# Six idle TensorE products fewer between the phases of the first pair of a fused SSD and FFN kernel

## Chip, cores and metric

The kernel runs on one core of one Trainium2 chip. The metric is the device time of one execution in microseconds (us); the median of five runs is compared. Next to it stands one profiled execution, whose records of every instruction make up the trace.

## What is computed

A Mamba-2 style state-space scan ("SSD") over batch 4, 8 heads, 768 positions, head width 32 and state width 16 is followed by a feed-forward network with squared ReLU. Cut to what matters:

```python
for c in range(S // 32):
    cum = cumsum(log(a[:, :, sl]))
    M   = (C_c @ B_c.T) * exp(cum_i - cum_j) * causal
    y[:, :, sl] = M @ x_c + (C_c @ state) * exp(cum)
    state = exp(cum_last) * state + sum_j(B_j x_j exp(cum_last - cum_j))
x = y.transpose(0, 2, 1, 3).reshape(3072, 256)
h = maximum(x @ w_in, 0)          # 256 -> 2048
out = (h * h) @ w_out             # 2048 -> 256
```

## The kernel before

The 768 positions of each batch element are cut into three stretches of 256. That gives twelve "pairs" (batch, stretch); the kernel numbers them 0 to 11, with all four batch elements of the first stretch first. A pair's SSD output is a tile T (bf16), and the feed-forward network runs over the same 256 positions: for each of eight steps, `mm1` (line 370, four products of 128x256, `hps`) then a ReLU on ScalarE (line 376), a square on VectorE (line 382) and `mm2` (line 400, four products, `ops`). `LAG = 4` steps lie between an `mm1` and its `mm2`.

All instructions are issued in the order in which the source lists them (`tc.manual_schedule()`): each engine goes through its own list strictly in that order, and waits where an operand is not ready. From pair 1 on, the SSD phases of a pair are threaded between the feed-forward steps of earlier pairs by a hand-written table of steps (`at(s, fn, ...)`). Pair 0 has no feed-forward work to stand beside, so its phases run one after another:

- the decays: VectorE scan `cp_r` (line 495), spread over partitions by TensorE products (`ctpt`, `ptr`, `pps`), scaled on VectorE into `bct` (line 526); ScalarE fills the rest of `bct` (line 524)
- `ph_mt(0)` (line 220): 16 products `mt` of B against C, 64x256, eight tiles of the array side by side
- the causal masks of `mt` on VectorE (`ph_mask`, line 231), half of them from a copy that ScalarE makes (`mtc`, line 545)
- `ph_u(0)` (line 249): 16 small products `U` for the carried state; they need `xs`, which GpSimd makes (line 176, `prep_x`)
- `ph_s(0, ...)`: ScalarE scales `U` into the state `Sf` (line 272)
- `ph_y(0)`: 8 products with the state (line 340), which need `Sf`, then 32 products of the masked `mt` with `xs` (line 307, `y_intra`), which need the masks
- two copies turn `Y` into `T0` (line 357), and `ph_tr(1)` starts pair 1 (lines 201 and 203)
- the first `mm1` (line 370)

Between these phases stand idle products, `warm(n, cols)`: n TensorE products of a zeroed tile `dum` with itself, `cols` columns wide, written to a PSUM tile that nobody reads. They wait for nothing and nobody waits for them, but TensorE goes through its list in order, so what is behind them starts only after them. Seven of them stand ahead of everything (lines 488 and 489, six of 512 columns and one of 256), the others are 256 columns wide.

The weights come in pieces on GpSimd's queue: `load_wi(0, 4)` (line 500), then after `prep_x(0)` `load_wi(4, 8)` (line 539), `load_wo(0, 4)` and `load_wo(4, 8)` (lines 548 and 549).

Of the kernel before, what the change touches and what calls it, by code (L numbers as in the profile page):

```python
# [16 lines left out]
def _fap(base: bass.AP, offset_elems: int, free_dims):  # L17

    ap0 = list(base.ap)[0]
    return bass.AP(tensor=base.tensor, offset=base.offset + offset_elems,  # L20
                   ap=[list(ap0)] + [list(d) for d in free_dims])
# [9 lines left out]
def kernel(  # L31
# [94 lines left out]
    def load_wi(f0, f1):  # L126

        for f in range(f0, f1, 2):
            nc.gpsimd.dma_start(  # L129
                out=w_in_b[:, :, f * 128:(f + 2) * 128],  # L130
                in_=_dap(moe_w_in, f * 128, [[2048, 128], [128 * 2048, 2], [1, 256]]))
# [81 lines left out]
    def ph_mt(k):  # L213
        v = live[k]
        bct = v["bct"]
        mt = [ps_s.tile([128, 2, 2, 2, 128], FP32, tag="A", name=f"mt{k}_{i}") for i in range(2)]
        for r in range(2):
            for u in range(2):
                for q in range(4):
                    nc.tensor.matmul(  # L220
                        mt[q // 2][64 * u:64 * u + 64, q % 2, r, :, :],
                        bct[32 * q:32 * q + 32, r, 0, u * 64:u * 64 + 64],
                        _fap(bct[32 * q:32 * q + 32], 128 + u * 64, [[128, 2], [384, 2], [1, 64]]),
                        start=True, stop=True, skip_group_check=True,
                        tile_position=(32 * q, 64 * u))
        v["mt"] = mt
        v["mts"] = big.tile([128, 4, 2, 2, 128], BF16, tag="mts", name=f"mts{k}")

    def ph_mask(k, q, src=None):
        v = live[k]  # L230
        nc.vector.tensor_tensor(  # L231
            out=v["mts"][:, q], in0=v["mt"][q // 2][:, q % 2] if src is None else src,
            in1=_fap(cb, 128, [[128, 2], [0, 2], [1, 128]]), op=ALU.mult)

    def ph_u(k):
        b, j = PAIRS[k]
        v = live[k]
        if k < 1:
            U = [ps_h.tile([128, 64], FP32, tag="hps", name=f"U{k}_{u}", padded_shape=[128, 512])
                 for u in range(2)]  # L240
        else:
            t = ps_s.tile([128, 2, 512], FP32, tag="A", name=f"U{k}")
            U = [t[:, u, 0:64] for u in range(2)]
        for r in range(2):
            for u in range(2):
                if j == 2 and u == 1:
                    continue
                for q in range(4):
                    nc.tensor.matmul(  # L249
                        U[u][32 * q:32 * q + 32, :],  # L250
                        v["Bb"][64 * u:64 * u + 64, r, 32 * q:32 * q + 32],
                        _fap(v["xs"][64 * u:64 * u + 64], r * 256 + q * 32, [[128, 2], [1, 32]]),
                        start=(r == 0), stop=(r == 1), skip_group_check=True,
                        tile_position=(64 * u, 32 * q))
        v["U"] = U
        v["S"] = [state.get(b)]
# [43 lines left out]
    def y_intra(k, Y, first, last):  # L300
        v = live[k]
        for g in range(2):
            for r in range(2):
                for u in range(2):
                    for q in range(4):
                        h = 4 * g + q
                        nc.tensor.matmul(  # L307
                            Y[u][32 * q:32 * q + 32, g, :],
                            v["xs"][64 * u:64 * u + 64, r, h * 32:h * 32 + 32],
                            v["mts"][64 * u:64 * u + 64, q, r, g, :],  # L310
                            start=first[(u, q)], stop=(last and g == 1 and r == 1), skip_group_check=True,
                            tile_position=(64 * u, 32 * q))
                        first[(u, q)] = False
# [3 lines left out]
    def ph_y(k):  # L317
        b, j = PAIRS[k]
        v = live[k]
        if k < 1:  # L320
            Y = [ps_s.tile([128, 2, 128], FP32, tag="A", name=f"Y{k}_{u}", padded_shape=[128, 8, 128])
                 for u in range(2)]
        else:
            t = ps_s.tile([128, 2, 4, 128], FP32, tag="A", name=f"Y{k}")
            Y = [t[:, u, 0:2, :] for u in range(2)]
        first = {(u, q): True for u in range(2) for q in range(4)}
        if 1 <= k < 4:
            y_intra(k, Y, first, False)
        for u in range(2):
            S_b = v["S"][u]  # L330
            if S_b is None:
                continue
            for g in range(2):
                rhs = [128 + g * 128 + u * 64, [[384, 2], [1, 64]]]
                if k >= 4:
                    nc.tensor.matmul(Y[u][:, g, :], S_b[:, g * 128:(g + 1) * 128], _fap(v["bct"], *rhs),  # L336
                                     start=first[(u, 0)], stop=False, skip_group_check=True)
                for q in range(4):
                    if k < 4:
                        nc.tensor.matmul(  # L340
                            Y[u][32 * q:32 * q + 32, g, :], S_b[32 * q:32 * q + 32, g * 32:(g + 1) * 32],
                            _fap(v["bct"][32 * q:32 * q + 32], *rhs),
                            start=first[(u, q)], stop=(k > 0 and g == 1), skip_group_check=True,
                            tile_position=(32 * q, 32 * q))
                    first[(u, q)] = False
        if k == 0:
            warm(2, 256)
        if k == 0 or k >= 4:
            y_intra(k, Y, first, True)
        if 4 <= k < NPAIR - 1:  # L350
            ph_u(k + 1)

        T[k] = tpool.tile([128, 2, 2, 2, 64], BF16, tag="T", name=f"T{k}")
        if k < 1:
            for u in range(2):
                copy = nc.vector.tensor_copy if u else nc.scalar.copy
                copy(out=_fap(T[k], u * 64, [[128, 4], [1, 64]]), in_=_fap(Y[u], 0, [[64, 4], [1, 64]]))
        else:
            nc.scalar.copy(out=_fap(T[k], 0, [[64, 2], [128, 4], [1, 64]]),  # L359
                           in_=_fap(Y[0], 0, [[512, 2], [64, 4], [1, 64]]))  # L360
# [84 lines left out]
    with tc.manual_schedule():  # L445
# [37 lines left out]
        def warm(n, cols=512):  # L483
            for _ in range(n):
                nc.tensor.matmul(idle[-1][:, 0:cols], dum[:, 0:128], dum[:, 0:cols],  # L485
                                 start=True, stop=True, skip_group_check=True)
# [50 lines left out]
        recip(0, 1, 0)  # L537
        prep_x(0, nc.gpsimd)
        load_wi(4, 8)
        warm(2, 256)  # L540
        ph_mt(0)
        warm(6, 256)
        mtc = {k: big.tile([128, 2, 2, 2, 128], BF16, tag="mtc", name=f"mtc{k}") for k in range(2)}
        for i in (1, 0):
            nc.scalar.copy(out=mtc[0][:, i], in_=live[0]["mt"][1][:, i])
# [2 lines left out]
        load_wo(0, 4)  # L548
        load_wo(4, 8)
        ph_u(0)  # L550
        warm(4, 256)
        ph_mask(0, 3, mtc[0][:, 1])
        ph_mask(0, 2, mtc[0][:, 0])
        prep_c(1, nc.vector)
# [3 lines left out]
        ph_s(0, (1,), "z")  # L558
        prep_b(1, nc.scalar)
        ph_y(0)  # L560
        ph_tr(1)
        recip(2, 2, 0)
# [45 lines left out]
        for k in range(2, NPAIR):  # L608
# [26 lines left out]
            else:  # L635
                if k == 4:
                    at(s0 + 4, ph_u, k)
                at(st + (5 if k == 4 else 0), ph_s, k)
            at(yy, ph_y, k)
        waiting = []  # L640
        between = {2: ((ph_u, (1,)), (ph_s, (1, (0,), "S"))), 3: ((ph_y, (1,)),)}
        for s in range(len(steps) + LAG):
            if s == 4:
# [43 lines left out]
```

## Time and profile before

| | us |
|---|---|
| median of five runs | 118.59 |
| the five runs | 117.41, 117.49, 118.59, 119.40, 119.50 |
| profiled execution, whole | 118.61 |
| its span, first to last instruction | 116.9 |

| engine | busy us | share of the span | instructions |
|---|---|---|---|
| TensorE products (PE) | 109.0 | 93% | 1639 |
| TensorE weight loads (PEld) | 88.0 | 75% | 1639 |
| VectorE (DVE) | 86.9 | 74% | 205 |
| ScalarE (ACT) | 76.2 | 65% | 145 |
| GpSimd (POOL) | 39.0 | 33% | 80 |

In the rows of a timeline the first number is the start in us from the span's beginning, the second the time to the end of the row's last instruction; then come engine, line, operation, output and inputs, shape and how many instructions the row stands for. A bracket tells how long the engine had been idle before and what released it. PE rows overlap, since the products are pipelined: a single 128x256 product is shown with 0.27 us, yet the next one starts much earlier, so the rate is read from the starts. The idle products are the rows of line 485 with the output `dps`.

### The profile page before, as it was taken

The page shows a single profiled execution, that of the slowest core. Times are in us where ns is not written, and L with a number is a line of the kernel's source. Part 1 is how long each engine was busy: PE and PEld are TensorE (multiplying, and loading weights), DVE is VectorE, ACT ScalarE, POOL GpSimd, SP SyncE. Part 2 cuts the span into 40 slices and gives each one's busy share as a digit, 9 for nine tenths or more (in the row PEclk, how much of TensorE's full clock was granted, in tenths as well). Part 3 has the DMA queues.
Part 4 walks back from the last instruction along what each step waited for, and adds up shares of the span by engine and source line. Part 5 has one row for each costly group of instructions (what it writes and reads, how often), then busy time and mean ns, then how long its engine had stood idle before and what let it go on. Part 6 is the DMA issues. An engine that isn't in the chain of part 4 may idle for free.

```text
span 116.9 us, 4011 instructions
## 1 busy us (share of the span) xinstructions
PE 109.0 (93%) x1639; PEld 88.0 (75%) x1639; DVE 86.9 (74%) x205; ACT 76.2 (65%) x145; POOL 39.0 (33%) x80
## 2 busy tenths in 40 slices
PE   5989889989999999999999999999999999999940
PEld 2555578777786787887887897887888878889940
DVE  6788936799796998996996976976958939554420
ACT  5465877576787566586576775865865775868710
POOL 4678966148792600431243604306100000000000
PEclk9999999999999999999999999999999999999999
DMA  3999999989899512927628639278050200200211
GB/s 73 192 169 144 148 193 185 190 138 202 151 286 196 104 48 68 208 68 143 149 95 157 95 97 203 42 172 167 11 157 0 83 12 0 93 2 0 90 48 48
DMA packets 50963, 13.53 MB, mean 116 GB/s; under 512 B 44352, under 2 KB 50048, under 8 KB 50944
## 3 DMA queue, kind: packets, MB, share of 16 engines
q1 hardware_dynamic: 46400, 10.98, 44.7%
q0 software_dynamic: 4288, 2.10, 14.3%
q8 instruction: 13, 0.21, 0.8%
q10 hardware_dynamic: 256, 0.18, 0.5%
q14 instruction: 6, 0.05, 0.1%
HBM read 10.64 MB, written 3.15 MB: 118 GB/s over the span
## 4 chain that ended last, share of the span: by engine, by line
PE 84%; DMA 5%; DVE 4%; POOL 2%; issue 0%; DVEq 0%
PE ops L400 35%; PE hps L370 33%; DMA w_out_b<-in_moe_w_out_dram 5%; PE mt L220 3%; PE Y L307 3%; PE dps L485 3%; DVE mts L231 2%; PE Y L336 2%; PE U L249 1%; POOL w_in_b L129 1%; POOL xs L176 1%; PE ctpt L509 1%; PE ops_r L400 1%; DVE bct L526 1%; PE ops L416 1%; PE ops_r L416 1%
## 5 line engine op out<-in xcount | busy, mean ns | idle before, releaser
L376 ACT ACTIVATE hb<-hps 128x512 bf16<-128x512 f32 x96 | 57.6, 600 | 29.9 <-PE hps L370 28.4
L370 PE MATMUL hps<-T,w_in_b 128*128 128x256 bf16 x384 | 57.6, 273 | 0.5 <-DMA w_in_b<-in_moe_w_in_dram 0.3
L400 PE MATMUL ops<-w_out_b,h 128*128 128x256 bf16 x360 | 55.0, 273 | 0.5 <-DMA w_out_b<-in_moe_w_out_dram 0.5
L382 DVE TENSOR_TENSOR h<-hb 128x512 bf16<-128x512 bf16 x96 | 41.2, 450 | 11.1 <-ACT hb L376 10.9
L370 PEld LDWEIGHTS <-w_in_b 128*128 128x128 bf16 x384 | 37.3, 98 | 5.1 <-DMA w_in_b<-in_moe_w_in_dram 0.6
L400 PEld LDWEIGHTS <-h 128*128 128x128 bf16 x376 | 34.5, 98 | 7.1 <-issue 2.6
L231 DVE TENSOR_TENSOR mts<-mt,cb 128x512 bf16<-128x512 f32 x44 | 29.1, 683 | 9.1 <-PE mt L220 9.0
L176 POOL TENSOR_TENSOR xs<-x_nat,Pinv 128x512 bf16<-128x512 f32 x12 | 13.2, 1100 | 10.9 <-DMA x_nat<-in_x_dram 3.2
L145 POOL TENSOR_TENSOR bc<-C_nat,P_sb 128x128 bf16<-128x128 f32 x16 | 6.8, 443 | 24.4 <-DMA C_nat<-in_C_dram 24.4
L293 DVE TENSOR_TENSOR S<-z,Pown 128x256 bf16<-128x256 f32 x16 | 8.1, 506 | 0.5
L485 PE MATMUL dps<-dum 128*128 128x256 bf16 (+1 forms) x25 | 6.3, 366 | 1.3 <-DVE dum L451 1.3
L359 ACT CAST T<-Y 128x512 bf16<-128x512 f32 x11 | 6.4, 585 | 0.4 <-PE Y L340 0.4
L438 ACT COPY osb<-ops 128x512 f32<-128x512 f32 x11 | 6.4, 580 | 0.0
L129 POOL DMA_DIRECT2D w_in_b<-in_moe_w_in_dram x8 | 6.0, 751 | 0.0
L220 PE MATMUL mt<-bct 32*64 32x256 bf16 x192 | 5.1, 280 | 0.5 <-DVE bct L526 0.3
L170 POOL CAST bc<-B_nat 128x128 bf16<-128x128 f32 x16 | 4.8, 326 | 2.0 <-DMA B_nat<-in_B_dram 2.0
L307 PE MATMUL Y<-mts,xs 64*32 64x128 bf16 x384 | 5.2, 219 | 0.0
L485 PEld LDWEIGHTS <-dum 128*128 128x128 bf16 x25 | 2.4, 112 | 3.3 <-issue 1.8
L307 PEld LDWEIGHTS <-xs 64*32 64x32 bf16 x384 | 3.0, 91 | 1.7 <-issue 0.8
L220 PEld LDWEIGHTS <-bct 32*64 32x64 bf16 x192 | 1.9, 102 | 3.2 <-issue 1.7
L286 DVE SCALAR_TENSOR_TENSOR z<-z,Ptot,U 128x64 f32<-128x64 f32 x12 | 3.2, 265 | 0.3 <-PE U L249 0.2
L134 POOL DMA_DIRECT2D w_out_b<-in_moe_w_out_dram x4 | 3.1, 790 | 0.3 <-issue 0.3
(77 smaller groups left out, 56.7 us busy)
## 6 DMA issues: line engine op xcount, KB each, us to landing
x_nat<-in_x_dram SPq DMA_DIRECT2D x12, 256.0 KB, 3.8
out_dram<-osb SPq DMA_DIRECT2D x7, 256.0 KB, 2.8
C_nat<-in_C_dram SPq DMA_DIRECT2D x12, 128.0 KB, 3.0
B_nat<-in_B_dram SPq DMA_DIRECT2D x12, 128.0 KB, 3.2
w_in_b<-in_moe_w_in_dram POOLq DMA_DIRECT2D x8, 128.0 KB, 5.5
w_out_b<-in_moe_w_out_dram POOLq DMA_DIRECT2D x4, 256.0 KB, 5.9
out_dram<-osb SPq DMA_DIRECT2D x8, 128.0 KB, 2.4
bct<-bc SPq DMA_TRANSPOSE x8, 3.5
```

The lines of the kernel that those rows point to most:

```text
L129: nc.gpsimd.dma_start(out=w_in_b[:, :, f * 128:(f + 2) * 128], in_=_dap(moe_w_in, f * 128, [[2048, 128], [128 * 2048, 2], [1, 256]]))
L145: eng.tensor_tensor(out=_fap(bc[k % 3], r * 384 + 128, [[144, 2], [32, 4], [1, 16]]), in0=_fap(loaded[k]["C"], r * 16, [[128, 2], [32, 4], ...
L176: eng.tensor_tensor(out=_fap(xs, 0, [[256, 2], [32, 8], [1, 32]]), in0=_fap(loaded[k]["x"], 0, [[32, 2], [64, 8], [1, 32]]), in1=_fap(Pinv ...
L220: nc.tensor.matmul(mt[q // 2][64 * u:64 * u + 64, q % 2, r, :, :], bct[32 * q:32 * q + 32, r, 0, u * 64:u * 64 + 64], _fap(bct[32 * q:32 * ...
L231: nc.vector.tensor_tensor(out=v["mts"][:, q], in0=v["mt"][q // 2][:, q % 2] if src is None else src, in1=_fap(cb, 128, [[128, 2], [0, 2], ...
L293: nc.vector.tensor_tensor(out=S_n.rearrange("p (g q d) -> p g q d", g=2, q=4), in0=_fap(z, 0, [[32, 2], [0, 4], [1, 32]]), in1=_fap(Pown, ...
L307: nc.tensor.matmul(Y[u][32 * q:32 * q + 32, g, :], v["xs"][64 * u:64 * u + 64, r, h * 32:h * 32 + 32], v["mts"][64 * u:64 * u + 64, q, r, ...
L370: nc.tensor.matmul(hps[:, i, :], w_in_b[:, g, f * 128:(f + 1) * 128], T[blk][:, g].rearrange("p r u t -> p (r u t)"), start=(g == 0), stop ...
L376: nc.scalar.activation(out=hb, in_=hps, func=AF.Relu)
L382: nc.vector.tensor_tensor(out=h2, in0=hb, in1=hb, op=ALU.mult)
L400: nc.tensor.matmul(o[c], h2[:, i, r * 128:(r + 1) * 128], w_out_b[:, f, c * 128:(c + 1) * 128] if len(o) > 1 else w_out_b[:, f, :], start= ...
L485: nc.tensor.matmul(idle[-1][:, 0:cols], dum[:, 0:128], dum[:, 0:cols], start=True, stop=True, skip_group_check=True)
```

## The change

Six of the idle products of 256 columns go: one of two ahead of `ph_mt(0)`, two of six behind it, two of four behind `ph_u(0)`, and one of two inside `ph_y(0)` between the products with the state and those of `y_intra`. Everything else, and its order on every engine, stays.

```diff
@@ ph_y, line 346
         if k == 0:
-            warm(2, 256)
+            warm(1, 256)
         if k == 0 or k >= 4:
             y_intra(k, Y, first, True)
@@ line 537
         recip(0, 1, 0)
         prep_x(0, nc.gpsimd)
         load_wi(4, 8)
-        warm(2, 256)
+        warm(1, 256)
         ph_mt(0)
-        warm(6, 256)
+        warm(4, 256)
@@ line 548
         load_wo(0, 4)
         load_wo(4, 8)
         ph_u(0)
-        warm(4, 256)
+        warm(2, 256)
         ph_mask(0, 3, mtc[0][:, 1])
```

## The prediction

> **What bounds the kernel now.** I read the page's row of the granted clock and its chain of waits first: TensorE (PE) carries 84% of the chain, in the two feed-forward lines above all, so whatever makes the first of these products start later is paid at the end, unless a later wait swallows it. So I went to the timeline of the first 16 us. PE's rows there, with the idle products (`dps`) among them:
>
> ```profile
> 1.26 2.96 PE L485 MATMUL dps<-dum 128*128 128x512 bf16 x7 [1.26 <-DVE dum L451]
> ...
> 6.21 0.38 PE L485 MATMUL dps<-dum 128*128 128x256 bf16 x2
> 6.89 0.42 PE L220 MATMUL mt<-bct 32*64 32x256 bf16 x16 [0.31 <-DVE bct L526]
> 7.25 0.83 PE L485 MATMUL dps<-dum 128*128 128x256 bf16 x6
> 8.11 0.25 PE L249 MATMUL U<-xs,Bb 64*32 64x64 bf16 x16
> 8.30 0.61 PE L485 MATMUL dps<-dum 128*128 128x256 bf16 x4
> 8.87 0.29 PE L340 MATMUL Y<-bct,Sf 32*32 32x128 bf16 x8
> 9.09 0.39 PE L485 MATMUL dps<-dum 128*128 128x256 bf16 x2
> 9.41 0.45 PE L307 MATMUL Y<-mts,xs 64*32 64x128 bf16 x32
> ...
> 10.54 0.60 PE L370 MATMUL hps<-T,w_in_b 128*128 128x256 bf16 x4
> ...
> 12.60 0.61 PE L370 MATMUL hps<-T,w_in_b 128*128 128x256 bf16 x4 [0.34 <-DMA w_in_b<-in_moe_w_in_dram]
> ...
> 15.10 0.60 PE L400 MATMUL ops<-w_out_b,h 128*128 128x256 bf16 x4 [0.49 <-DMA w_out_b<-in_moe_w_out_dram]
> ```
>
> What each real phase waits for, on the other engines:
>
> ```profile
> 5.87 0.88 DVE L526 SCALAR_TENSOR_TENSOR bct<-ctpt,half,P_T 128x256 bf16<-128x256 f32 x2
> 7.00 1.06 POOL L176 TENSOR_TENSOR xs<-x_nat,Pinv 128x512 bf16<-128x512 f32 x1 [0.74 <-DVE Pinv L534]
> 8.50 0.31 ACT L272 ACTIVATE Sf<-U,Ptot 128x64 bf16<-128x64 f32 x1
> 8.64 0.75 DVE L231 TENSOR_TENSOR mts<-mtc,cb 128x512 bf16<-128x512 bf16 x2
> ```
>
> **Two rates of one product.** The seven leading products (six of 512 columns, one of 256, so 13 half-widths) run from 1.26; the weight loads of line 485 start 0.427 us apart there (1.66, 2.09, 2.52, 2.94, 3.37). That is 0.213 us for 256 columns. The six at 7.25 take (0.83 - 0.27) / 5 = 0.11 us each, 0.27 being one product's own length (the page's 273 ns). So this execution ran at half rate first and at full rate by 7.25. The page's clock row, all nines, does not show it; the trace's clock records hold one full-clock stretch, from 4.98 to 117.62 us. In another execution full clock can come at another moment, and no row here shows such a one. The five runs do spread over 2.1 us (117.41 to 119.50), so both cases have to be worked out.
>
> **At full clock, as profiled, each edit costs and brings nothing.** Each group ends before what PE waits for anyway:
> - two ahead of `mt`: 6.21 + 0.22 = 6.43; `bct` is written until 5.87 + 0.88 = 6.75
> - six behind it: 7.25 + 6 x 0.11 = 7.91; `xs` is there at 7.00 + 1.06 = 8.06
> - four behind `U`: 8.30 + 0.44 = 8.74; `Sf` at 8.50 + 0.31 = 8.81
> - two ahead of the masked products: 9.09 + 0.22 = 9.31; the masks at 8.64 + 0.75 = 9.39
>
> So 6 x 0.11 = 0.66 us of PE work goes and 0.66 us of waiting takes its place. The cover is thin (0.07 to 0.32 us), which is why the rate decides. Nothing is queued differently on VectorE, ScalarE, GpSimd or SyncE: no wait is added, no transfer is moved. `xs` hangs on `Pinv`, thus on VectorE, and the weights' issues behind it on GpSimd's list, not on an idle product.
>
> **At half clock throughout the pair, step by step.** I keep the other engines' durations and give PE 0.213 us for each idle product. For `mt` half rate adds between 0 and 0.21 us (16 products of 256 columns on eight tiles are two rounds, each 0.107 longer; at full rate it takes 0.36 from start to the next start, more than its two rounds of 0.11, so issue limits part of it); I take 0.15, so PE is done with `mt` at 7.40 and the masked products could start at 9.41 + 0.15 = 9.56, as VectorE's masks follow `mt`. `U` and the state products (0.19 and 0.22) I leave, being 64 and 128 columns wide; that is low by at most 0.2 together, and equally in both kernels.
> - before `mt`: 6.21 + 0.43 = 6.64, still under 6.75. Removing one: 0.
> - `U` starts at 7.40 + 6 x 0.213 = 8.68 instead of 8.06; with four, at 8.25.
> - `Sf` lets the state products start 0.76 behind `U` (8.11 to 8.87): 9.44 before, 9.01 after. PE itself is free at 8.68 + 0.19 + 4 x 0.213 = 9.72 before and at 8.25 + 0.19 + 2 x 0.213 = 8.87 after. They start at 9.72 and 9.01.
> - the masked products: 9.72 + 0.22 + 2 x 0.213 = 10.37 before; 9.01 + 0.22 + 0.21 = 9.44 after, which then wait for the masks until 9.56.
>
> Sum: 10.37 - 9.56 = 0.81 us earlier, with the waits on `Sf` and the masks as what is late next. The choice for `mt` does not matter: with 0.21 it is 10.43 against 9.62, with 0 it is 10.22 against 9.41. `T`, its copies and the first feed-forward products follow one for one.
>
> **What of it is left at the end.** The 0.81 us has to pass two gates: `w_in` (0.34 us of PE waiting at 12.60) and `w_out` (0.49 us at 15.10). They swallow it if PE arrives early there. At half clock it does not: from 10.54 to 15.10, four groups of line 370 cost 4 x (0.85 - 0.44) = 1.64 more, three idle products 0.31, `mt` and `Y` of pair 1 some 0.3; less the waits of 0.34 + 0.49 and of about 0.2 ahead of `mt`, PE is 1.2 late at the second gate plus what pair 0 left. Then the lead survives. But if full clock comes at a moment of its own and not after so much work, 0.81 us of work at half rate is worth 0.40 at full rate. So an execution with late full clock gains 0.4 to 0.8, one with early full clock 0. Nothing shows which share of runs is late; the median (118.59) is 1.2 above the fastest run, so I count it as late, and as the trace gives the clock a moment I take the lower end of the gain, 0.4: 118.59 - 0.4 = 118.2. The profiled execution (118.61, of which 1.7 lie outside its span) would itself keep its time.
>
> [...] The trace's full clock began 3.7 us after PE's first product and ended 5.1 us after its last (112.5 to 117.62). [...]
>
> **Rivals.**
> - *Nothing happens (118.6).* All executions have full clock by 6 us, as the profiled one; the spread comes from transfers (PE stands 0.83 us at the two gates). For it: every cover above holds at full rate. Against it: 2.1 us is more than both gates together.
> - *Slower: full clock comes later (120.1).* At half clock the new kernel leaves PE idle 0.14 ahead of the state products (9.01 - 8.87) and 0.12 ahead of the masked ones (9.56 - 9.44), where the old one left nothing. If that is too little activity, runs that had full clock near 8 us keep half clock past 15 us. Price: the 1.2 above plus about 0.3 in pair 0: 1.5, so 118.59 + 1.5 = 120.1. It decides once more than half of the executions fall there. For it: PE's first full clock followed nearly gapless work. Against it: a clock that is full is not lost by this, since PE's half-empty last stretch and 5 us of nothing were needed for that, and 0.3 us of gaps is little.
> - *Clearly faster (117.2).* The lead of 0.81 counts in full in the median run, and dense products that start earlier bring full clock earlier, so that two groups of line 370 more run at 0.44 instead of 0.85 us (0.82): 118.59 - 1.6 is 117.0, and I stop a little above, 117.2, near the fastest run shown (117.41). For it: 117.41 exists, so the kernel has such a state. Against it: no row ties the clock's moment to these products.
>
> **How the numbers follow.** Forecast (0 to 0.8 less) 0.29, nothing 0.15, slower 0.30, clearly faster 0.26. A change of over 1% is 1.2 us, about what measuring this kernel can tell from none, given its spread. The first two stay within, and so does a little of each of the others: faster 0.25, same 0.47, slower 0.28. The range reaches from 116.9 (just under the faster case) to 120.1 (the slower case): it leaves out half of the slower case and little else. The likeliest case's own range is 117.8 to 118.6.
>
> **What would show it.** In the changed profile: at full clock, `mt`, `U`, the state products and the masked products start at 6.89, 8.11, 8.87 and 9.41 still, with gaps of PE ahead of them that are 0.1, 0.2, 0.2 and 0.1 longer, and `ops` waits for `w_out` at about 15.1. If idle products stand 0.21 apart after 6 us, the masked products should start at 9.5 to 9.7. The prediction is wrong if idle products stand 0.21 apart where they stood 0.11 apart before and the first product of line 370 starts later than 10.54 for it, or if a phase waits for something not in the lists above.

## Result and profile after

The change makes no difference that these runs can tell: 118.73 us median over 44 runs against 118.59 us over 79 runs of the kernel before, ratio 1.0008 with a 95% interval of 0.9987 to 1.0030. That is between 0.15 us less and 0.36 us more; the 0.4 us less that the prediction named as likeliest is just outside. The medians are over all runs; the ratios here and below compare only the runs that lie within 1.5% of the fastest run of their kernel.

The profiled execution took 117.72 us, its span is 116.0 us. PE's rows in the timeline of its first 15 us, to be laid beside those of before:

```profile
6.02 0.27 PE L485 MATMUL dps<-dum 128*128 128x256 bf16 x1
6.70 0.42 PE L220 MATMUL mt<-bct 32*64 32x256 bf16 x16 [0.41 <-DVE bct L526]
7.06 0.61 PE L485 MATMUL dps<-dum 128*128 128x256 bf16 x4
7.92 0.26 PE L249 MATMUL U<-xs,Bb 64*32 64x64 bf16 x16 [0.25 <-POOL xs L176]
8.11 0.39 PE L485 MATMUL dps<-dum 128*128 128x256 bf16 x2
8.67 0.29 PE L340 MATMUL Y<-bct,Sf 32*32 32x128 bf16 x8 [0.18 <-ACT Sf L272]
8.90 0.28 PE L485 MATMUL dps<-dum 128*128 128x256 bf16 x1
9.11 0.56 PE L307 MATMUL Y<-mts,xs 64*32 64x128 bf16 x32
...
10.35 0.60 PE L370 MATMUL hps<-T,w_in_b 128*128 128x256 bf16 x4
...
14.93 0.60 PE L400 MATMUL ops<-w_out_b,h 128*128 128x256 bf16 x4 [0.66 <-DMA w_out_b<-in_moe_w_out_dram]
```

The six products are gone, and what PE waits for stands in the brackets instead: `xs` (0.25 us idle), `Sf` (0.18), `bct` (0.41 instead of 0.31). From `mt` to the first product of line 370 it is 3.65 us both times (6.89 to 10.54, 6.70 to 10.35). All of it lies 0.19 us earlier because this execution's clock records show full clock from 4.58 us instead of 4.98, so that the products of line 509 ended sooner. At the weights' gate that lead is 0.17 us (14.93 against 15.10).

The 0.9 us between the two profiled spans is not the change's. PE's last product ends at 112.52 us before and at 112.77 after. What follows is the landing of the last stores, by the lists of DMA issues (queue, issues, size of each, us from issue to landing). Before:

```profile
out_dram<-osb ACTq DMA_DIRECT2D x1, 128.0 KB, 3.1
out_dram<-osb SPq DMA_DIRECT2D x2, 64.0 KB, 2.8
```

After:

```profile
out_dram<-osb ACTq DMA_DIRECT2D x1, 128.0 KB, 1.9
out_dram<-osb SPq DMA_DIRECT2D x2, 64.0 KB, 1.7
```

The stores landed 1.1 to 1.2 us faster, in instructions that the change does not touch. A single profiled span is therefore no measure of an edit of this size.

### The profile page after: what moved, and what is told of

It reads as the page before. It is cut to its first block, busy times and chain, and to the rows that moved or that the text cites. A ratio compares the mean times of both kernels' runs of the same rounds, so it can differ in the third digit from the quotient of the medians.

```text
span 116.0 us, 3999 instructions
## 1 busy us (share of the span) xinstructions
PE 108.4 (93%) x1633; PEld 87.6 (75%) x1633; DVE 88.2 (76%) x205; ACT 76.1 (66%) x145; POOL 39.1 (34%) x80
## 4 chain that ended last, share of the span: by engine, by line
PE 81%; DVE 8%; DMA 5%; POOL 2%; issue 1%; DVEq 0%
PE ops L400 34%; PE hps L370 32%; DMA w_out_b<-in_moe_w_out_dram 5%; DVE mts L231 3%; PE mt L220 3%; PE Y L307 3%; PE dps L485 3%; DVE h L382 2%; PE Y L336 2%; POOL w_in_b L129 1%; PE U L249 1%; POOL xs L176 1%; PE ops_r L400 1%; DVE bct L526 1%; PE ops L416 1%; PE ctpt L509 1%
## 5 line engine op out<-in xcount | busy, mean ns | idle before, releaser
L382 DVE TENSOR_TENSOR h<-hb 128x512 bf16<-128x512 bf16 x96 | 43.3, 474 | 11.2 <-ACT hb L376 11.1
L293 DVE TENSOR_TENSOR S<-z,Pown 128x256 bf16<-128x256 f32 x16 | 7.3, 458 | 0.5
L485 PE MATMUL dps<-dum 128*128 128x256 bf16 (+1 forms) x19 | 5.6, 396 | 1.3 <-DVE dum L451 1.3
```

Source lines behind the costliest of these rows:

```text
L293: nc.vector.tensor_tensor(out=S_n.rearrange("p (g q d) -> p g q d", g=2, q=4), in0=_fap(z, 0, [[32, 2], [0, 4], [1, 32]]), in1=_fap(Pown, ...
L382: nc.vector.tensor_tensor(out=h2, in0=hb, in1=hb, op=ALU.mult)
```

## Experiments

My theory was: at full clock the products are hidden; at half clock they delay pair 0 by about 0.8 us; and since the kernel's runs spread over 2 us, a median run is one of the late kind. The result speaks against the last part or against the gain reaching the end. The rivals: half clock does not happen; it happens, but later waits swallow it; the idle products hold the clock and so give as much as they cost.

**Profiling again.** The two kernels unchanged, one more profiled execution of each:

> The kernel before, profiled once more. Theory (full clock comes early as a rule): the six products behind mt stand 0.11 us apart again, the masked products start by 9.6 us. Rival (half clock is common): the products behind mt stand 0.21 apart and the masked products start at 10.2 to 10.5 us.

> The changed kernel, profiled once more. If it has full clock early (4 to 5 us), mt, U, the state products and the masked products start near 6.7, 7.9, 8.7 and 9.1 us again; if full clock comes near 10 us, as in the second profile of before, they start near 7.3, 8.7, 9.5 and 10.1, the masked products 0.6 to 0.8 us earlier than the 10.79 there. In both cases the mm1 products at the seventh step of the second four-step round start between 25.9 and 26.6 us.

The kernel before, in this second profile, had full clock only from 9.87 us (clock records). PE's rows of the timeline:

```profile
7.96 1.46 PE L485 MATMUL dps<-dum 128*128 128x256 bf16 x6
9.35 0.31 PE L249 MATMUL U<-xs,Bb 64*32 64x64 bf16 x16
9.59 0.73 PE L485 MATMUL dps<-dum 128*128 128x256 bf16 x4
10.25 0.29 PE L340 MATMUL Y<-bct,Sf 32*32 32x128 bf16 x8
10.47 0.39 PE L485 MATMUL dps<-dum 128*128 128x256 bf16 x2
10.79 0.42 PE L307 MATMUL Y<-mts,xs 64*32 64x128 bf16 x32
...
15.76 0.61 PE L400 MATMUL ops<-w_out_b,h 128*128 128x256 bf16 x4
```

So half clock through pair 0 does happen. The six idle products take 1.46 us instead of 0.83, no phase waits for its operand any more (no brackets), and the masked products start at 10.79 instead of 9.41, 1.38 late. Nor does PE wait for `w_out`. Yet this execution took 117.95 us, less than the median.

The changed kernel, profiled again, had full clock from 4.54 us and took 117.93 us:

```profile
9.09 0.56 PE L307 MATMUL Y<-mts,xs 64*32 64x128 bf16 x32
...
15.89 0.27 PE L400 MATMUL ops<-w_out_b,h 128*128 128x256 bf16 x1 [1.60 <-DVE h L382]
```

Here the masked products started 1.70 us earlier than in the profile at half clock, and the products of line 400 0.13 us later: PE stood idle for 1.60 us ahead of them. The releaser named is a square, the fourth, which ended at 15.89. But these products read the first step's square, and the first three had ended by 14.45; in the first profile after the change the same products started at 14.93, ahead of the fourth square (15.44 to 15.86). What else they read is `w_out`, and its first piece is the cause: it was issued at 9.27 and landed 6.58 us later, at 15.85, 0.04 us before PE went on. In both first profiles, where the releaser named is `w_out`, PE also went on 0.04 us behind the landing (15.06 and 15.10 before, 14.88 and 14.93 after). The two executions differ by 1.70 us in pair 0 and by 0.02 us at the end.

**Where a delay goes.** From the rows of line 370 in each trace, the start of a step's four products (steps counted from 0), in us:

| execution | masked products | step 0 | step 4 | step 12 | step 14 | last step |
|---|---|---|---|---|---|---|
| before | 9.41 | 10.54 | 15.54 | 23.67 | 26.20 | 109.71 |
| before, second profile (half clock to 9.87) | 10.79 | 11.91 | 16.52 | 24.50 | 26.58 | 110.17 |
| after | 9.11 | 10.35 | 15.36 | 23.35 | 26.34 | 109.96 |
| after, second profile | 9.09 | 10.33 | 16.32 | 24.31 | 26.62 | 110.15 |

The 1.38 us of the half-clock profile are 0.98 behind the weights' gate, 0.83 at step 12 and 0.38 at step 14. The lead of 0.30 that the first profile after the change has in the masked products is 0.32 at step 12 and turns into 0.14 of lag at step 14. Between those steps lies a third gate, the `U` products of pair 2, which wait for VectorE's masks of pair 2 (`U` goes into a PSUM buffer that `mt` held, so the masks must have read it). The row of these products before:

```profile
24.69 0.26 PE L249 MATMUL U<-xs,Bb 64*32 64x64 bf16 x16 [0.42 <-DVE mts L231]
```

In the second profile of before:

```profile
25.08 0.25 PE L249 MATMUL U<-xs,Bb 64*32 64x64 bf16 x16
```

After the change:

```profile
24.83 0.26 PE L249 MATMUL U<-xs,Bb 64*32 64x64 bf16 x16 [0.88 <-DVE mts L231]
```

So PE waited 0.42 us there before, 0.88 us after, and in the half-clock profile not at all. From step 14 to the last step all four take 83.5 to 83.6 us, so nothing more is won or lost there.

**Twice and four times the idle products,** which puts a known delay into pair 0 at full clock:

```diff
-warm(2), mt, warm(6), U, warm(4), state products, warm(2)     # 256 columns each
+warm(4), mt, warm(12), U, warm(8), state products, warm(4)    # e2_double
+warm(8), mt, warm(24), U, warm(16), state products, warm(8)   # e5_quad
```

> The idle products of pair 0 behind the leading seven are doubled (2, 6, 4, 2 become 4, 12, 8, 4), which at full clock is what half clock makes of the old number: 12 x 0.11 = 1.32 us behind mt put U at 8.57 instead of 8.11, the state products at 9.64 and the masked products at 10.30 instead of 9.41 us, 0.89 late. Theory (gates): the waits for w_in (0.34 us at 12.6) and for w_out (0.49 to 0.66 us at 15) swallow most of it, the products of line 400 still start within 0.3 us of 15.1, and the time rises by 0 to 0.3 us (118.6 to 118.9). Rival (one for one): PE is the bound, so the whole 0.89 us is paid: 119.5.

> The idle products of pair 0 behind the leading seven are made four times as many (8, 24, 16, 8). At full clock 24 x 0.11 = 2.64 us behind mt put U at 9.9, the state products at 11.8 and the masked products at 12.9 instead of 9.4 us: 3.5 late. Theory (gates): what PE waits for anyway takes its part once, 0.34 us at w_in, 0.49 to 0.66 at w_out and 0.4 to 0.9 at the masks of pair 2 near 24.7 us, 1.2 to 1.9 in all, and nothing more; so the time rises by 1.6 to 2.3 us (about 120.2 to 120.9). Rival (one for one): 3.5 us are paid. Rival (PE has slack everywhere): under 1 us is paid.

Doubled: 118.71 us, ratio 1.0029 (0.9990 to 1.0068), which is 0.34 us more. The masked products started at 10.61, 1.2 us late, 0.3 more than I had worked out. PE still waited for `w_out`:

```profile
15.94 0.60 PE L400 MATMUL ops<-w_out_b,h 128*128 128x256 bf16 x4 [0.30 <-DMA w_out_b<-in_moe_w_out_dram]
```

That is 0.8 us later than I expected, since the transfer itself took 6.40 us from issue to landing in this execution against 5.58 in the first profile of before: the gate moves from execution to execution by as much as the effect at issue. Four times as many: 120.76 us over four runs, ratio 1.0216 (1.0153 to 1.0280), 2.6 us more (1.8 to 3.3), for 4.2 us in pair 0, where I had worked out 3.5:

```profile
13.60 0.42 PE L307 MATMUL Y<-mts,xs 64*32 64x128 bf16 x32
```

So by the times 1.6 us were swallowed, and the interval allows 0.9 to 2.4. The profiles are sharper: against the first profile of before, the doubled kernel's 1.19 us are 0.25 at step 14 (26.45), and the 4.19 us here are 3.42 (29.62). The start-up thus swallows 0.8 to 1.0 us in each of the three profiles with a delay, less than the 1.2 to 1.9 that I had summed from the gates, and the rest is paid.

**Half clock forced.** Without the seven leading products PE begins at 4.2 to 4.4 us, and full clock comes later (at 10.21 to 13.54 us in the three profiles). With the counts of before, of after, and with none behind them:

```diff
-        warm(6)
-        warm(1, 256)
```

> The seven leading idle products are left out, the others stand as before the change (2, 6, 4, 2). PE's first product is then that of line 509 at about 4.3 us, so full clock should come some 3 us later than the 4.6 to 5.0 us of the two profiles, between 7.5 and 11.5 us. Theory (half clock delays pair 0): idle products stand 0.21 us apart behind mt, U starts at 8.6 to 8.9, the masked products at 10.2 to 10.6 instead of 9.1 to 9.4 us; the time is 0.5 to 1.5 us longer than before. Rival (gates): all of pair 0's delay is swallowed by the wait for w_out at 15: time within 0.3 us of before, even so.

> The same without the seven leading products, with the idle products of the changed kernel (1, 4, 2, 1). Theory (half clock delays pair 0): the masked products start 0.6 to 0.9 us earlier than in the run without leading products and with 2, 6, 4, 2, and the time is 0.4 to 0.8 us shorter than there. Rival (gates): both start the products of line 400 at about 15, and the two times are equal within 0.3 us. [...]

> Neither the seven leading idle products nor the 14 behind them in pair 0. Theory: at half clock the products of the changed kernel end with the waits, so leaving them out moves no phase of pair 0 forward by more than 0.2 us against the run without leading products and with 1, 4, 2, 1 (masked products at 9.9 to 10.2); what is left is the clock: full clock begins later, near 14 to 17 us instead of 13.2, and the time is 0 to 1 us longer than there. Rival (idle products do nothing for the clock): full clock begins between 10 and 13.5 us and the time is the same within 0.3 us.

| idle products of pair 0 behind the leading seven (left out) | full clock from | masked products | step 14 | median us | ratio to before |
|---|---|---|---|---|---|
| 2, 6, 4, 2 | 10.21 | 11.02 | 26.81 | 119.27 | 1.0075 (1.0030 to 1.0119) |
| 1, 4, 2, 1 | 13.21 | 10.11 | 26.78 | 118.53 | 1.0035 (1.0003 to 1.0067) |
| none | 13.54 | 9.59 | 27.07 | 118.39 | 1.0019 (0.9979 to 1.0059) |

In pair 0 the theory holds: with the changed counts the masked products start 0.91 us earlier than with those of before, in the one profile of each. Of that, 0.18 is the start of the first product (4.21 against 4.39), so 0.73 is the idle products'. The two rows of the timeline with the changed counts in which state and masked products can be read:

```profile
9.45 0.40 PE L340 MATMUL Y<-bct,Sf 32*32 32x128 bf16 x8
...
10.11 0.63 PE L307 MATMUL Y<-mts,xs 64*32 64x128 bf16 x32
```

At step 14 the two profiles are equal all the same (26.78 and 26.81), and the last step comes later with the changed counts (110.82 against 110.27). The times say otherwise. Set directly against each other, the runs of the first two rows that the ratios count have means of 119.09 us (nine runs) and 118.48 us (twelve), 0.61 us apart; an estimate from their spread puts the difference at 0.1 to 1.1 us. So at forced half clock fewer idle products are faster in the times, as the theory expects, but the one profile of each does not show where. Without any idle product the masked products start another 0.5 us earlier, which I had put at no more than 0.2: at half clock even the changed counts do not quite end with the waits.

The last row deserves attention. A kernel with none of the 21 idle products ahead of and inside pair 0 takes the time of before within its interval, 118.39 against 118.36 us in the same comparison.

**Do the idle products hold the clock?** With the leading seven, and none or four behind them:

```diff
-warm(2), mt, warm(6), U, warm(4), state products, warm(2)
+mt, U, state products                          # e1_none
+mt, warm(3), U, warm(1), state products        # e7_four
```

> All 14 idle products of 256 columns in pair 0 behind the leading seven are left out (2, 6, 4, 2 become 0). Theory (hidden): at full clock they stand in waits that end at 6.75 (bct), 8.06 (xs), 8.81 (Sf) and 9.39 us (masks), so the time stays at 118.6 within 0.3 us, and mt, U, the state products and the masked products start where they did, with PE gaps of 0.5, 0.7, 0.5 and 0.3 us ahead of them. Rival (clock): these products hold or bring the full clock; without them idle gaps add up to 2 us within 3.4 us, full clock comes later in many executions, and the time rises by 1.0 to 1.5 us (119.6 to 120.1). Rival (half clock is common): then the gain of the change is a part of what can be had, and this kernel gains 0.4 us or more (118.2 or less).

> With the leading seven, only four idle products are left in pair 0: three behind mt and one behind U (0, 3, 1, 0). Theory (products hold the clock, by number): executions whose mean granted clock is 0.991 or less were 5 of 35 with 14 such products, 6 of 44 with eight and 8 of 12 with none; with four it is in between, 3 to 7 of 12, and the time is 0 to 0.4 us above before. Rival (only none is too few): at most 2 of 12.

With none: 118.67 us, ratio 1.0052 (1.0016 to 1.0087), 0.6 us more. Neither the theory (0.3 us at most) nor the rival (1.0 at least) had that. But over all runs of this comparison the medians are 118.67 and 118.27 us and the means 118.62 and 118.67, since the times of before reach from 117.02 to 124.06 us and these only from 118.07 to 119.24. Whether this kernel is slower at all is not settled. The windows of its profile, cut at the times of the clock records (length, then busy us of PE, PEld, DVE, ACT and POOL with instructions, granted clock, DMA share, GB/s):

```profile
0.65:4.06 3.41, 2.80 (x7) 0.89 (x7) 2.85 (x11) 2.08 (x4) 1.81 (x7) 1.00 0.67 123
4.06:7.47 3.41, 2.20 (x29) 1.66 (x29) 2.47 (x9) 1.69 (x7) 2.40 (x4) 1.00 1.11 188
7.47:10.88 3.41, 2.46 (x64) 1.66 (x64) 2.94 (x9) 2.12 (x7) 3.41 (x6) 0.50 1.10 164
10.88:14.30 3.42, 3.42 (x30) 1.84 (x28) 2.57 (x6) 2.27 (x4) 2.89 (x7) 0.50 1.17 126
```

The first row's 1.00 is a gap of the record, not a measurement: the leading products in it stand 0.427 us apart, and full clock is on record from 4.06 only. It lasts to 7.47, and then half clock is granted until 14.30, after a stretch in which PE was busy for 2.20 of 3.41 us. The rows of PE show it in the same products that took 0.45 and 0.60 us before:

```profile
9.06 0.85 PE L307 MATMUL Y<-mts,xs 64*32 64x128 bf16 x32
...
10.67 1.06 PE L370 MATMUL hps<-T,w_in_b 128*128 128x256 bf16 x4
```

So in this kernel the idle products do hold the clock, and the rival is right in this much. Executions with a mean granted clock of 0.991 or less: 9 of 75 with fourteen of them (the runs of before that went with these experiments), 6 of 44 with eight, 6 of 12 with four, 8 of 12 with none. (A late first full clock does not count here: nothing is recorded ahead of it, and the half-clock profile of before has a mean of 0.998.) But no price of it shows in the times. With none, the eight executions that lost full clock for a while took 118.64 us in the mean and the other four 118.60. With four, the time is 118.46 us, ratio 0.9999 (0.9958 to 1.0040), although half of its executions lost it. In the profile with none, at half clock from 7.47 to 14.30 us, step 14 starts at 26.65, where it does in the two second profiles of the table, though the last step comes at 110.63, 0.5 us behind theirs.

The fifteen executions of that kind with fourteen or eight idle products are another matter: they took 119.04 to 124.06 us. None of them was profiled, so it is not known whether they lost the clock in the start-up or later, and the shares above need not count the same thing.

**The third gate taken away,** in the kernel before:

```diff
-            2: (9, 12, 12, 10, (10, 11, 11, 12), 14),
+            2: (9, 13, 13, 10, (10, 11, 11, 12), 14),
```

> The kernel before, with the products U of pair 2 and the ScalarE steps behind them one step later in the hand-written table (12 becomes 13). In the profile before, PE waited 0.42 us for pair 2's masks ahead of these products at 24.69 us, in the profile of the change 0.88 us; in the second profile of before, which was at half clock until 9.9 us, it did not wait there. Theory (this wait is one of those that swallow pair 0's delay or lead, and what PE does not wait there it gains): without it the mm1 products of the steps behind start 0.2 to 0.4 us earlier (25.8 to 26.0 instead of 26.20) and the time falls by 0.1 to 0.4 us. Rival (VectorE's masks bound this stretch): the wait turns up again ahead of the products Y of pair 2 near 26.7 us, and the time stays within 0.1 us.

118.70 us, ratio 1.0009 (0.9966 to 1.0051). In its timeline PE does not wait ahead of these products, nor ahead of `Y` of pair 2:

```profile
25.41 0.25 PE L249 MATMUL U<-xs,Bb 64*32 64x64 bf16 x16
26.67 0.42 PE L307 MATMUL Y<-mts,xs 64*32 64x128 bf16 x32
```

From step 12 to step 14 it took 2.14 us (24.00 to 26.14) instead of 2.53, so the wait is gone and not replaced there. It came into this stretch 0.33 us later than the first profile of before, so step 14 missed the 25.8 to 26.0 expected. That profile stood 0.49 us at the weights' gate, and this one 0.81 us. The interval allows 0.4 us of gain and 0.6 of loss: whether the time fell is not settled. No kernel tried here beats before or after measurably.

## Why the prediction was right, and where not

- **At full clock the six products are hidden: right.** Both profiles of the change show the waits of the prediction, on `xs`, `Sf`, `bct`, where the products had been.
- **Half clock delays pair 0 by about 0.8 us: right in place, near in size.** The second profile of before has the masked products at 10.79 (predicted 10.37; everything ahead of `mt` was at half rate too, which I had left out: `mt` started at 7.38 instead of 6.89). The changed counts with full clock from 13.21 have them at 10.11 (predicted 9.56), 0.68 earlier; against the same kernel with the counts of before it is 0.73.
- **"So I count it as late": wrong, the step that cost the forecast its 0.4 us.** Full clock began between 4.06 and 6.36 us in eight of the nine profiles of kernels that keep the leading products, and near 10 us in one. And the one late execution took 117.95 us, less than the median. So the spread of the runs gives no sign of half clock in pair 0. What is seen to vary are landings: the first piece of `w_out` took 5.58 to 6.58 us, the last stores 1.9 or 3.1 us; that these make the whole spread is not shown.
- **"Then the lead survives": in part at most.** I had counted two gates and found PE late at both, the second by 1.2 us because the feed-forward products would run at half rate up to there. In the late profile they did not: full clock came at 9.87, ahead of their first start at 11.91. And there is a third gate: PE stood up to 0.88 us at pair 2's masks near 24.7 us, and of 1.38 us of delay 0.38 was left at step 14. By the profiles an execution at half clock can thus gain about 0.4 us; by the times at forced half clock it is 0.6 us (0.1 to 1.1), so how much survives is open. With one in nine of that kind, which rests on a single execution, the mean gain is an estimated 0.04 to 0.07 us, far below the interval.
- **"Nothing happens (118.6)" is the rival that came true,** and its reason holds nearly: full clock came by 6.4 us in eight of nine profiles, not in all. That the result lies in my range is luck as far as the half-clock step goes: the range from 116.9 to 120.1 was wide enough for no effect at all.
- **"Slower: full clock comes later" has a real mechanism,** shown with four and with no idle products behind the leading seven (6 and 8 of 12 executions with a mean granted clock of 0.991 or less), but eight of them leave the share where fourteen do (6 of 44 against 9 of 75), and its price of 1.5 us does not show: with none, the executions that lost full clock were 0.04 us longer in the mean than the others. Its two moments, near 8 and past 15 us, no run shows: full clock began at 4.06 to 6.36 us or near 10 with the leading products and at 10.21 to 13.54 without them, and in the profile with none behind the leading seven, which lost it at 7.47, it was back at 14.30.
- **"Clearly faster"** needed a median run at half clock and a lead that reaches the end in full; the profiles show neither. That dense products that start earlier bring full clock earlier is not shown either: without the leading products those of line 370 began at 11.49 with the changed counts and at 12.14 with those of before, and full clock came 3.00 us later (13.21 against 10.21).

## What to carry to other kernels

Before pricing an edit in a prologue, follow a delay of known size (twice and four times the suspected work) to the first step behind the last wait of the start-up; only what is left there counts. Here 0.8 to 1.0 us of every delay was gone by then, taken by a weights' landing and another engine's chain. Idle products that keep a clock up are worth what the clock is worth in that stretch: this start-up waits for transfers and masks anyway, and with all 21 gone neither they nor the later full clock showed in the time (118.39 against 118.36 us).

## What was not expected of the hardware

- Full clock can be taken back while PE works. In the profile with no idle products behind the leading seven it was granted at 4.06, gone at 7.47, back at 14.30: on for 3.41 us, off for 6.83. In the 3.41 us ahead of the loss PE was busy for 2.20. The profile with four idle products kept full clock, with PE busy for 2.59 us of 4.11 to 7.52 and for 2.50 us of 7.52 to 10.93. How little work loses the clock, two profiles do not settle.
- A busy PE is not enough to get it. Without the leading products, and with the counts of before, PE shows work in all of 6.80 to 10.21 us, and full clock came at 10.21. With the changed counts PE shows work in all of 6.39 to 9.80 us, and full clock still came only at 13.21. Of the 51 products of that stretch 40 (`mt`, `U` and `Y`) are 32*64, 64*32 or 32*32 in the rows, where an idle product is 128*128; which property counts, these runs do not tell.
- A square on VectorE, 0.42 us in the median of its line, took 1.32 us beside a GpSimd multiplication that began 0.02 us earlier. From the timeline after the change:

```profile
22.74 1.06 POOL L176 TENSOR_TENSOR xs<-x_nat,Pinv 128x512 bf16<-128x512 f32 x1 [2.93 <-DMA x_nat<-in_x_dram]
22.76 1.32 DVE L382 TENSOR_TENSOR h<-hb 128x512 bf16<-128x512 bf16 x1
```

Before, the multiplication came behind the square, which took its usual time:

```profile
23.08 0.42 DVE L382 TENSOR_TENSOR h<-hb 128x512 bf16<-128x512 bf16 x1
23.58 1.06 POOL L176 TENSOR_TENSOR xs<-x_nat,Pinv 128x512 bf16<-128x512 f32 x1 [2.71 <-DVE h L382]
```

After the change the square ended at 24.08, 0.28 us behind the multiplication, and pair 2's masks came behind it: that is why PE waited 0.88 us at the third gate instead of 0.42. Seven more squares with a row of their own in this trace began while a multiplication of line 176 ran (at 32.30, 35.48, 40.65, 50.20, 65.83, 74.19 and 82.42): they took 0.52 to 1.12 us and ended 0.27 to 0.29 us behind it as well. Two that began 0.04 and 0.23 us ahead of one (34.55 and 49.27) took 0.41. Why the square is held up, the rows do not show.
